# An attention and gated-convolution kernel: q and k of the first batch element in six tensors, the first w_in tile in one piece

## The chip, the cores and the metric

One core of a Trainium2 chip runs the program. The metric is the device time of one execution in microseconds (us), the median over runs; a profiled execution gives the trace. The engines are TensorE (PE), VectorE (DVE), ScalarE (ACT), GpSimd (POOL) and SyncE (SP), which here only issues DMAs.

## The reference

Block-causal attention (blocks of 64) over 8 batch elements, 8 heads, 576 positions and head size 64, and behind it a feed-forward layer with a gate from a convolution of three taps over positions:

```python
scores = scale * q @ k.T;  mask by blocks of 64;  attn = softmax(scores)
x = (attn @ v), heads side by side                      # 8 x 576 x 512
h = np.maximum(x @ w_in, 0.0)                           # 512 -> 1024
conv_out[s] = sum over j of conv_w[j] * h[s + j - 1]    # zero outside 0..575
gate = 1.0 / (1.0 + np.exp(-conv_out))
return (h * gate @ w_out).astype(np.float32)            # 1024 -> 512
```

q, k, v are float32. w_in, conv_w and w_out are float64: the kernel reads them as pairs of 32-bit words and puts float32 values together on the chip ("decode").

## The kernel before, in words

**Precision.** Most products run on pairs of a high part (type fp32r) and a low remainder: weights stand as wih and wil (w_in) and woh and wol (w_out). Heads are handled in pairs, four pairs per batch element.

**The decode of a weight tile** (function `split`, which calls `decode`). w_in has eight tiles of 128 columns, 512 KB each as 64-bit words. A tile is loaded (L1142), then: absolute value (ACT, L1013), clamp (L1019, POOL, for tile 0 DVE), a shift (DVE, L1024), the sign put in (DVE, L1036), a mask (DVE, L1040), then the high part (ACT, L1082) and a first low part (DVE, L1047). PE forms minus the high part and plus that low part in a bank (L1098, L1101), and DVE adds the value (L1104), which gives wil. Staging buffers gh and gl hold two tiles each. Before the change tile 0 is the one that is cut in two halves (`SHARE = {0: 2}`), so that each step of it runs twice on half the width; tile 1 comes first.

**The first batch element** is done in two visits per pair: "A" for its first 256 positions, for all four pairs, then "B" for the rest. The later elements are one visit per pair, 28 in all. For the A visits `load_first` fetches 256 positions of q and k of all pairs in twelve DMAs (L952): for q and for k a group for pair 0, one for pair 1 and one for pairs 2 and 3, each in two loads of 128 positions. The two loads of k for pair 0 go by ACT's queue, the rest by SP's. They all land in one tensor, seen under two types (`qkf`, `qkr`):

```python
qkt = [nc.alloc_sbuf_tensor_at(f"qk{x}", [P, 2, 2, H, D], d, offset=at0).ap() for x, d in (("f", F32), ("r", F32R))]
```

`first_t` then transposes a pair's q or k on PE (two matmuls, L1326) and ACT copies the result out (L840). Scores follow (L1578, with the mask L1582), row maxima (DVE, L1596), exponentials (ACT, L1604), sums and reciprocals (DVE, L1610, L1614), scaling (POOL, L1619), transposes of the probabilities (PE, L1665) and the product with v.

The feed-forward products are L1867 (w_in) and L1933 (w_out); they fill PE wherever attention leaves room.

**The order** is not written by hand. Every operation has a due time in a table of numbers (TARGETS), and `Plan.order` simulates the five engines with fixed costs per operation: on each engine the ready operation with the lowest due time goes next. Where the planner sees PE without work it puts in filler matmuls (L2085) whose result is not used. The planner knows for a transpose only the loads of its own group (`deps=lds[p]`). The semaphore waits are set by the framework from the tensors that an instruction reads and writes. DMA completions go round eight semaphores, so a DMA also waits until the one eight places before it has landed.

Of the kernel before, what the change touches and what calls it, by code (L numbers as in the profile page):

```python
# [11 lines left out]
F32 = mybir.dt.float32  # L12
F32R = mybir.dt.float32r
# [568 lines left out]
def kernel(  # L582
# [10 lines left out]
    nc = tc.nc  # L593
# [3 lines left out]
    P = 128  # L597
# [59 lines left out]
    VAT = (0, 1, None, 0)  # L657
    SRAW, PRA, PRB = True, True, (0, 1)
    FHP = ()
    ZDMA, APM, SHARE = True, True, {0: 2}  # L660
    LQ, LQS, LV, LVS = -60.0, 8.22, -56.75, 13.33
    WL0, WLS = -49.08, 2.41
    NEAR, FAR, BIAS = 0.0, 1.0, 0.0
# [277 lines left out]
    def load_first():  # L941
# [25 lines left out]
        for z in range(2):  # L967
            res.append((lambda z=z: qkt[1][:, z], bufs, lds[z]))
# [1153 lines left out]
```

## Time and profile before

| | us |
|---|---|
| median of 3 runs | 766.57 (766.47 to 767.78) |
| profiled execution | 767.02 |
| its span | 765.2 |
| PE busy | 748.2 (98% of the span) |
| DVE busy | 628.4 (82%) |
| ACT busy | 605.2 (79%) |
| POOL busy | 426.7 (56%) |

The span runs from the first to the last instruction. Matmuls overlap in the pipeline and the ends are modelled, so a busy PE is not a PE at its peak; fillers count as busy. A row of a stage gives each engine's busy time in that stretch, with the number of its instructions. The chain of waits is followed back from the last instruction and is shown in order of time: start, length, and what ran or landed. A row "A <- B: total, times, longest" is a wait of A for B. A row of a group gives the count, the busy time, the mean of one in ns and the idle time ahead.

### The profile page before, as it was taken

How to read it: one execution, taken by the hardware profiler on the slowest of the kernel's cores; microseconds unless marked ns; L12 is line 12 of the kernel's file. 1: busy time of each engine (PE TensorE's matmuls, PEld its weight loads, DVE VectorE, ACT ScalarE, POOL GpSimd, SP SyncE). 2: the span in 40 equal slices, each digit the busy share in tenths (PEclk: the TensorE clock that was granted, in tenths of full speed). 3: DMA queues.
4: the chain of work that ended last, by engine and by line, in shares of the span. 5: the costliest groups of instructions: out<-in, count | busy, mean ns of one | idle time of the engine just before them, and what ended most of it. 6: DMA issues, size and time to landing. Idle time of an engine off the chain costs nothing.

```text
span 765.2 us, 16814 instructions
## 1 busy us (share of the span) xinstructions
PE 748.2 (98%) x5175; PEld 672.3 (88%) x5175; DVE 628.4 (82%) x1840; ACT 605.2 (79%) x1754; POOL 426.7 (56%) x642
## 2 busy tenths in 40 slices
PE   6999999999999999999999999999999999999998
PEld 4666789989989899999989899898989899898997
DVE  3899999989978789898979789798888879786541
ACT  2888989978978679797978689798888768786652
POOL 1444765766755547576566547546566655564421
PEclk9999999999999999999999999999999999999999
DMA  7575574667544565645354663555456454440001
GB/s 198 149 181 149 126 167 116 152 163 167 127 104 113 126 144 120 142 113 136 94 135 113 142 151 93 136 124 130 103 117 156 106 147 102 95 102 15 14 29 42
DMA packets 165629, 92.64 MB, mean 121 GB/s; under 512 B 134924, under 2 KB 142116, under 8 KB 165540
## 3 DMA queue, kind: packets, MB, share of 16 engines
q1 hardware_dynamic: 164996, 91.43, 49.3%
q8 instruction: 42, 0.69, 0.4%
q14 instruction: 47, 0.39, 0.2%
q10 hardware_dynamic: 544, 0.13, 0.1%
HBM read 38.30 MB, written 9.44 MB: 62 GB/s over the span
## 4 chain that ended last, share of the span: by engine, by line
PE 77%; ACT 11%; DVE 5%; DMA 3%; issue 2%; POOL 1%; SPq 0%; ACTq 0%; DVEq 0%; POOLq 0%
PE bank L1933 25%; PE bank L1867 21%; PE bank L1785 10%; PE bank L1665 6%; PE bank L1470 4%; PE bank L1472 4%; PE bank L1423 3%; PE bank L1216 2%; DMA qkf<-in_k_dram 2%; DMA x<-in_moe_w_out_dram 2%; ACT ptbh L1676 1%; DVE st L1480 1%; ACT p4f L1439 1%; DVE t L1888 1%; ACT t L1884 1%
## 5 line engine op out<-in xcount | busy, mean ns | idle before, releaser
L1867 PE MATMUL bank<-x,wih 128*128 128x290 f32 (+3 forms) x1024 | 199.3, 299 | 0.0
L1907 POOL TENSOR_TENSOR gl<-t,gh 128x289 fp32r<-128x289 f32 (+3 forms) x128 | 104.1, 819 | 102.8 <-ACT gh L1904 97.4
L1867 PEld LDWEIGHTS bank<-x,wih 128*128 128x128 f32 x1024 | 157.6, 188 | 3.5 <-issue 0.4
L1933 PE MATMUL bank<-woh,gh 128*128 128x512 f32 (+1 forms) x296 | 118.2, 399 | 0.0
L1933 PE MATMUL bank<-wol,gh 128*128 128x512 f32 (+1 forms) x296 | 115.0, 389 | 0.0
L1933 PE MATMUL bank<-woh,gl 128*128 128x512 f32 (+1 forms) x296 | 114.9, 388 | 0.0
L1867 PE MATMUL bank<-x,wil 128*128 128x290 f32 (+3 forms) x512 | 110.7, 298 | 0.0
L1480 DVE TENSOR_REDUCE st<-bank 128x1 f32<-128x128 f32 (+3 forms) x224 | 106.5, 481 | 2.8
L1676 ACT ACTIVATE ptbh<-bank 128x384 fp32r<-128x384 f32 (+2 forms) x180 | 87.1, 503 | 11.6 <-PE bank L1665 10.7
L1679 DVE TENSOR_TENSOR ptbl<-bank,ptbh 128x512 fp32r<-128x512 f32 (+1 forms) x142 | 88.7, 632 | 8.0 <-ACT ptbh L1676 5.7
L1888 DVE SCALAR_TENSOR_TENSOR t<-bank,cw,t 128x289 f32<-128x289 f32 (+3 forms) x128 | 65.0, 509 | 25.6 <-ACT t L1884 25.1
L1867 PEld LDWEIGHTS bank<-x,wil 128*128 128x128 f32 x512 | 82.5, 188 | 1.0
L835 POOL TENSOR_SCALAR vv<-vn 128x320 fp32r<-128x320 f32 (+2 forms) x62 | 28.5, 461 | 82.1 <-DMA vn<-in_v_dram 29.3
L1472 PE MATMUL bank<-kl,qz 128*128 128x128 f32 (+2 forms) x224 | 71.7, 322 | 0.0
L1884 ACT ACTIVATE t<-bank,cw 128x289 f32<-128x289 f32 (+3 forms) x128 | 63.9, 500 | 5.0 <-POOL gl L1907 2.7
L1933 PEld LDWEIGHTS bank<-woh,gl 128*128 128x128 f32 x296 | 55.5, 188 | 12.5
L1892 DVE SCALAR_TENSOR_TENSOR t<-bank,cw,t 128x288 f32<-128x288 f32 (+3 forms) x128 | 64.5, 506 | 1.3
L1785 PE MATMUL bank<-ptbl,vv 128*64 128x192 f32 x240 | 64.5, 314 | 0.0
L1904 ACT ACTIVATE gh<-t 128x289 fp32r<-128x289 f32 (+3 forms) x128 | 56.7, 445 | 9.8 <-DVE t L1900 8.8
L1897 ACT ACTIVATE t<-t 128x289 f32<-128x289 f32 (+3 forms) x128 | 56.8, 444 | 8.9 <-DVE t L1892 8.2
L1881 ACT ACTIVATE bank<-bank 128x290 f32<-128x290 f32 (+3 forms) x128 | 51.6, 403 | 14.5 <-PE bank L1867 12.7
L1900 DVE SCALAR_TENSOR_TENSOR t<-t,bank 128x289 f32<-128x289 f32 (+3 forms) x128 | 57.0, 446 | 6.0 <-ACT t L1897 4.9
(183 smaller groups left out, 2013.4 us busy)
## 6 DMA issues: line engine op xcount, KB each, us to landing
out_dram<-stage SPq DMA_DIRECT2D x35, 256.0 KB, 2.3
ka<-kh SPq DMA_DIRECT2D x56, 144.0 KB, 2.6
kb<-kh SPq DMA_DIRECT2D x56, 144.0 KB, 2.6
vn<-in_v_dram SPq DMA_DIRECT2D x60, 128.0 KB, 2.7
qnf<-in_q_dram SPq DMA_DIRECT2D x56, 128.0 KB, 2.4
knf<-in_k_dram SPq DMA_DIRECT2D x56, 128.0 KB, 2.7
x<-in_moe_w_out_dram SPq DMA_DIRECT2D x8, 512.0 KB, 4.0
qz<-qh SPq DMA_DIRECT2D x28, 144.0 KB, 2.5
```

Source lines behind the costliest of these rows:

```text
L1472: nc.tensor.matmul(sb.ap[:, 0:nk], qz.ap[:, z:z + 128], kl.ap[:, 0:nk], start=False, stop=True)
L1480: nc.vector.tensor_reduce(out=st.ap[:, i:i + 1], in_=sb.ap[:, 0:nk], op=ALU.max, axis=AX.X, negate=True)
L1676: nc.scalar.activation(out=hi(), in_=src(), func=AF.Copy)
L1679: nc.vector.tensor_tensor(out=lo(), in0=src(), in1=hi(), op=ALU.subtract)
L1785: nc.tensor.matmul(tb.ap[0:m, q0 - qa:qb - qa], vv.ap[:, chunk(c), w[ps_]], pm.ap[:, 128 * c + q0:128 * c + qb] if qa == 0 else pm.ap[:, c ...
L1867: nc.tensor.matmul(fb.ap[:, 0:n2], wt[:, c, fs], xs[c][xi].ap[:, x0:x0 + n2], start=(n + c - c0 == 0), stop=(n + c - c0 == 3 * NCC - 1))
L1884: nc.scalar.activation(out=t.ap[:, 0:no], in_=fb.ap[:, own:own + no], func=AF.Copy, scale=cw[:, NFC + f:NFC + f + 1])
L1888: nc.vector.scalar_tensor_tensor(out=t.ap[:, i0:no], in0=fb.ap[:, own + i0 - 1:own + no - 1], scalar=cw[:, f:f + 1], in1=t.ap[:, i0:no], o ...
L1892: nc.vector.scalar_tensor_tensor(out=t.ap[:, 0:i1], in0=fb.ap[:, own + 1:own + 1 + i1], scalar=cw[:, 2 * NFC + f:2 * NFC + f + 1], in1=t.a ...
L1900: nc.vector.scalar_tensor_tensor(out=t.ap[:, 0:no], in0=t.ap[:, 0:no], scalar=1.0, in1=fb.ap[:, own:own + no], op0=ALU.add, op1=ALU.mult)
L1907: nc.gpsimd.tensor_tensor(out=gbuf[1].ap[:, f, carry:carry + no], in0=t.ap[:, 0:no], in1=gbuf[0].ap[:, f, carry:carry + no], op=ALU.subtract)
L1933: nc.tensor.matmul(fb.ap[:, 0:cut], gbuf[a].ap[:, f, cs], w[:, f, ds], start=(f == 0 and n == 0), stop=(f == NFC - 1 and n == 2))
```

## The change: six tensors, one piece, and another table of due times

The one tensor of q and k becomes six, each under two types: for q and for k one for pair 0, one for pair 1 and one for pairs 2 and 3. Loads and transposes address their own. They lie at the same place in memory, one behind the other. Tile 0 of w_in is no longer cut. TARGETS is another table of 6,414 numbers in place of 6,425, since the uncut tile has fewer operations. Below line 734 line numbers rise by five (L1326 becomes L1331).

```diff
-219 209 325 302 354 325 246 281 286 295 371 375 506 444 710 738 354 406 519 734 553 576 526 591 650 559 328 325 411 393 578 563 408 432 411 482 459 473 436
...
-    ZDMA, APM, SHARE = True, True, {0: 2}
+    ZDMA, APM, SHARE = True, True, {}
...
-    qkt = [nc.alloc_sbuf_tensor_at(f"qk{x}", [P, 2, 2, H, D], d, offset=at0).ap() for x, d in (("f", F32), ("r", F32R))]
+    qkt = [[[], []], [[], []]]
+    for z in range(2):
+        for p0, p1 in ((0, 1), (1, 2), (2, 4)):
+            for y, (x, d) in enumerate((("f", F32), ("r", F32R))):
+                qkt[y][z].append(nc.alloc_sbuf_tensor_at(f"qk{x}{z}{p0}", [P, 2, 2 * (p1 - p0), D], d, offset=at0).ap())
+            at0 += 4 * 4 * (p1 - p0) * D
...
-                        eng.dma_start(out=qkt[0][:, z, c, 2 * p0:2 * p1, :],
+                        eng.dma_start(out=qkt[0][z][g][:, c],
...
-            res.append((lambda z=z: qkt[1][:, z], bufs, lds[z]))
+            res.append((lambda z=z: qkt[1][z], bufs, lds[z]))
...
-                                     x()[:, c, 2 * p:2 * p + 2, :].rearrange("p j d -> p (j d)"), rident, start=(c == 0), stop=True,
+                                     x()[min(p, 2)][:, c, 2 * (p == 3):2 * (p == 3) + 2, :].rearrange("p j d -> p (j d)"), rident, start=(c == 0), stop=True,
```

**PE at the start.** Here is the start of PE's queue before, with the semaphores on which each instruction waits; DMAHW0 to DMAHW7 are the eight of the DMAs.

```order
L2085 MATMUL bank<-blank 128x512 x13
L1326 MATMUL bank<-rident,qkr 128x128 [waits DMAHW2_49,DMAHW3_49,DMAHW1_49,DMAHW4_49,DMAHW0_49,DMAHW7_49,DVE_49,PE_49]
L1326 MATMUL bank<-rident,qkr 128x128
L2085 MATMUL bank<-rident 128x512 x7
L1098 MATMUL bank<-wih,nident 128x512 [waits PE_49,Activation_49]
L1101 MATMUL bank<-wil,rident 128x512 [waits DVE_49]
L2085 MATMUL bank<-rident 128x512 [waits PE_49]
L2085 MATMUL bank<-rident 128x512 x2
L1098 MATMUL bank<-wih,nident 128x256 [waits PE_49,Activation_49]
L1326 MATMUL bank<-rident,qkr 128x128 [waits DMAHW3_49,DMAHW4_49,DMAHW2_49,DMAHW6_49,DMAHW0_49,DVE_49]
L1326 MATMUL bank<-rident,qkr 128x128 x3
L1578 MATMUL bank<-kh,qa 128x128 [waits Activation_49]
```

And now (qkr10 is k of pair 0, qkr00 q of pair 0, qkr01 q of pair 1):

```order
L2090 MATMUL bank_165<-blank_141 128x512 x17
L1103 MATMUL bank_208<-wih_136,nident_132 128x512 [waits PE_49,Activation_49]
L1331 MATMUL bank_211<-rident_130,qkr10_120 128x128 [waits DMAHW2_49,DMAHW0_49,DVE_49]
L1331 MATMUL bank_211<-rident_130,qkr10_120 128x128
L1106 MATMUL bank_208<-wil_137,rident_130 128x512 [waits DVE_49]
L2090 MATMUL bank_220<-rident_130 128x512 x5
L1103 MATMUL bank_233<-wih_136,nident_132 128x512 [waits DVE_49,Activation_49]
L1331 MATMUL bank_236<-rident_130,qkr00_114 128x128 [waits DMAHW6_49,DMAHW4_49,PE_49]
L1331 MATMUL bank_236<-rident_130,qkr00_114 128x128
L1106 MATMUL bank_233<-wil_137,rident_130 128x512 [waits DVE_49]
L1331 MATMUL bank_245<-rident_130,qkr01_116 128x128 [waits DMAHW7_49,DMAHW0_49,PE_49]
```

A transpose waits for two DMA semaphores instead of five or six, the fillers at the front are 18 instead of 14 (one more row of one stands ahead of each), and the transposes of q stand behind products of two w_in tiles. In all there are 34 fillers instead of 36.

**SP at the start.** SP's queue before, and behind it the queue now:

```order
L952 DMA qkf<-in_k_dram 128x2x64
L952 DMA qkf<-in_k_dram 128x2x64 [waits DMAHW0_49]
L952 DMA qkf<-in_q_dram 128x2x64 [waits DMAHW1_49]
L952 DMA qkf<-in_q_dram 128x2x64 [waits DMAHW2_49,PE_49]
L952 DMA qkf<-in_q_dram 128x4x64 [waits DMAHW3_49]
L952 DMA qkf<-in_q_dram 128x4x64 [waits DMAHW4_49]
L1184 DMA t<-in_moe_conv_w_dram 24x256 [waits DMAHW5_49]
```

```order
L1147 DMA gh<-in_moe_w_in_dram 128x4x256 x2
L957 DMA qkf_113<-in_q_dram 128x2x64
L1147 DMA gl<-in_moe_w_in_dram 128x4x256
L957 DMA qkf_113<-in_q_dram 128x2x64
L957 DMA qkf_115<-in_q_dram 128x2x64
L957 DMA qkf_115<-in_q_dram 128x2x64 [waits DMAHW0_49]
L1189 DMA t<-in_moe_conv_w_dram 24x256 [waits DMAHW1_49]
L957 DMA qkf_121<-in_k_dram 128x2x64 [waits DMAHW2_49]
L957 DMA qkf_121<-in_k_dram 128x2x64 [waits DMAHW3_49]
L957 DMA qkf_117<-in_q_dram 128x4x64 [waits DMAHW4_49]
```

The wait for PE at the fourth row of before is gone; the loads of q for pair 0 stand behind two and three whole w_in tiles (before, behind one; half a tile and another whole one followed). Further on, tile 7 of w_in waits in this queue for DVE, and the next loads of q and k for the B visits stand behind it.

**DVE at the start.** DVE's queue now, from the first w_in tile on:

```order
L1029 TENSOR_SCALAR gh<-gh 128x512
L1041 SCALAR_TENSOR_TENSOR gh<-gh 128x512
L1045 TENSOR_SCALAR gh<-gh 128x512
L1024 TENSOR_SCALAR gh<-gh 128x512
L1052 SCALAR_TENSOR_TENSOR wil<-gh 128x4x128
L1029 TENSOR_SCALAR gh<-gh 128x512
L1041 SCALAR_TENSOR_TENSOR gh<-gh 128x512
L1109 TENSOR_TENSOR wil<-bank,gh 128x4x128
L1045 TENSOR_SCALAR gh<-gh 128x512
L1052 SCALAR_TENSOR_TENSOR wil<-gh 128x4x128
L1109 TENSOR_TENSOR wil<-bank,gh 128x4x128
L1029 TENSOR_SCALAR gl<-gl 128x512
```

The steps of the first two tiles are woven together and both stand ahead of the third (gl); before, the second set was half of tile 0, its last step stood behind the first two maxima of pair 0, and tile 0's other half followed behind tile 3.

More of the change, by code (lines that the diff above doesn't have):

```diff
@@ L949, in load_first, with go @@
                 for c in range(2):
-                    def go(src=src, z=z, c=c, p0=p0, p1=p1):
+                    def go(src=src, z=z, c=c, p0=p0, p1=p1, g=g):
                         eng = nc.scalar if src is k and p0 == 0 else nc.sync
-                        eng.dma_start(out=qkt[0][:, z, c, 2 * p0:2 * p1, :],
+                        eng.dma_start(out=qkt[0][z][g][:, c],
                                       in_=src[0, 2 * p0:2 * p1, 128 * c:128 * c + 128, :].rearrange("h p d -> p h d"))
@@ L1326, in tr @@
                     nc.tensor.matmul(tb.ap[:, c * P:(c + 1) * P].bitcast(F32R),
-                                     x()[:, c, 2 * p:2 * p + 2, :].rearrange("p j d -> p (j d)"), rident, start=(c == 0), stop=True,
+                                     x()[min(p, 2)][:, c, 2 * (p == 3):2 * (p == 3) + 2, :].rearrange("p j d -> p (j d)"), rident, start=(c == 0), stop=True,
                                      is_transpose=True, skip_group_check=True)
```

435 rows, old and new, of the table TARGETS are left out of this document.

## The prediction

> **What bounds the kernel now.** I read the page's sums first, then the stages, then the chain of waits at the start.
>
> ```profile
> span 765.2 us, 16814 instructions
> PE 748.2 (98%) x5175; PEld 672.3 (88%) x5175; DVE 628.4 (82%) x1840; ACT 605.2 (79%) x1754; POOL 426.7 (56%) x642
> 0.00:20.00 20.00, 12.45 (x46) 9.12 (x47) 6.36 (x22) 5.70 (x12) 2.20 (x8) 0.90 0.72 200
> 20.00:45.00 25.00, 23.34 (x142) 15.30 (x142) 22.82 (x68) 22.50 (x74) 10.63 (x23) 0.95 0.65 174
> 45.00:60.00 15.00, 14.84 (x91) 10.36 (x91) 14.21 (x35) 12.96 (x38) 6.68 (x9) 1.00 0.66 167
> 60.00:100.00 40.00, 38.53 (x255) 29.38 (x254) 36.50 (x94) 35.73 (x102) 24.45 (x36) 1.00 0.54 135
> 100.00:700.00 600.00, 596.81 (x4269) 551.95 (x4268) 523.97 (x1573) 497.05 (x1456) 365.09 (x547) 1.00 0.52 124
> 0.00:20.00 20.00, 9.56 (x24) 6.81 (x24) 0.90 0.72 200
> 20.00:45.00 25.00, 5.27 (x12) 2.66 (x12) 0.95 0.65 174
> ```
>
> The first two lines are the page's; then stages with, after the length, the busy time of PE, PEld, DVE, ACT and POOL, the granted clock, the DMA share and GB/s; the last two count the filler matmuls (L2085) alone. From 100 to 700 us PE is busy 596.81 of 600, so the end is PE's work plus whatever PE loses before. It loses nearly all at the start: in 0 to 100 us it idles 100 - 89.16 = 10.84 us (the four stages sum to 89.16) and runs 9.56 + 5.27 = 14.83 us of fillers, 25.7 us together. In the first 20 us DVE works 6.36 and ACT 5.70 us; from 20 to 45 us DVE works 22.82 and ACT 22.50 of 25. So the start is slow because something late keeps DVE and ACT from their backlog. The chain says what:
>
> ```profile
> 0.73 3.78 DMA qkf<-in_k_dram
> 4.53 4.39 DMA qkf<-in_k_dram
> 9.42 0.48 PE bank L1326 x2
> 9.91 0.37 SPq L952
> ...
> 12.92 4.71 DMA qkf<-in_k_dram
> 17.72 0.36 PE bank L1326 x2
> PE bank L1326 <- DMA qkf<-in_k_dram: 6.0, 2, 3.3
> SPq L952 <- PE bank L1326: 4.4, 1, 4.4
> ```
>
> Columns: start, length; in the two wait rows the total, the times, the longest. The first transposes (L1326, pair 0's q) run at 9.42, just behind a load of k for pair 1 that lands at 4.53 + 4.39 = 8.92, though their own q stands second in SP's queue. SP's next q load waits for these transposes (4.4 us), so everything behind it in SP's queue leaves from 9.91 on. The second transposes wait for the last of all twelve loads, 12.92 + 4.71 = 17.63. Both rows fit one cause: q and k are one tensor, so a reader waits for every load issued to it, and a load waits for every reader.
>
> **The change part by part.** *Six tensors.* Each transpose now waits for its own two loads, and no q or k load waits for PE. PE's 6.0 us and SP's 4.4 us go. What is late next are loads, or the weight decode that PE's queue has ahead of the transposes. These rows price it:
>
> ```profile
> 2.00:4.00 2.00, 2.00 (x6) 1.54 (x5) 0.00 (x0) 1.10 (x1) 0.00 (x0) 1.00 0.91 277
> 4.00:6.00 2.00, 2.00 (x6) 1.53 (x6) 0.00 (x0) 1.02 (x3) 0.35 (x1) 1.00 1.06 251
> 6.00:8.00 2.00, 0.65 (x3) 0.19 (x1) 1.54 (x3) 0.00 (x0) 0.26 (x1) 1.00 1.03 316
> 1.05 5.60 PE L2085 MATMUL bank<-blank 128*128 128x512 f32 x14 [1.05 <-DVE blank L829]
> 6.76 0.69 DVE L1036 SCALAR_TENSOR_TENSOR gh<-gh 128x512 int32<-128x512 int32 x1
> 7.55 0.43 DVE L1040 TENSOR_SCALAR gh<-gh 128x512 int32<-128x512 int32 x1
> 10.53 0.62 ACT L1082 ACTIVATE wih<-gh 128x512 fp32r<-128x512 f32 x1
> 10.87 0.69 DVE L1047 SCALAR_TENSOR_TENSOR wil<-gh 128x512 fp32r<-128x512 uint32 x1
> 13.29 0.69 DVE L1104 TENSOR_TENSOR wil<-bank,gh 128x512 fp32r<-128x512 f32 x1 [1.07 <-PE bank L1101]
> 18.54 0.49 PE L1578 MATMUL bank<-kh,qa 64*128 64x128 f32 x4 [0.31 <-ACT kh L840]
> 24.19 1.13 DVE L1596 TENSOR_REDUCE st<-bank 128x1 f32<-128x128 f32 x4
> 24.28 0.38 POOL L1619 TENSOR_SCALAR p0f<-p0f,st 128x128 f32<-128x128 f32 x1 [11.58 <-DVE t L1040]
> 24.63 0.48 POOL L1619 TENSOR_SCALAR p1f<-p1f,st 128x256 f32<-128x256 f32 x1
> 24.95 0.25 PE L1665 MATMUL bank<-rident,p0r 128*128 128x128 f32 x1 [0.15 <-ACT qa L840]
> 27.52 0.57 ACT p1f L1604 x2
> 28.16 0.35 ACT p0f L1604 x2
> ```
>
> Loads: the first three rows move 554 + 502 + 632 KB by 8 us. Ahead of pair 0's second q load now stand k (128 KB), three whole w_in tiles (1,536) and half of q (64), so with its own 64 it is done after 1,792 KB, about 8.5 us; pair 1's q at 9.0 and k at 9.7, pair 2's q at about 11. The second tile is there after 1,152 KB, at 6.5.
>
> PE's queue: 18 fillers now stand first; at 5.60/14 = 0.40 each they end near 8.3. Then two decodes are woven in. DVE has the first tile's steps at the times shown until 7.98; then come, by the shown lengths, the second tile's clamp (0.43) to 8.4, the first's low part (0.69) to 9.1, and the second's steps (0.43, 0.69) to 10.2, its high part on ACT (0.62) to 10.9, DVE's remainder of the first (0.69) to 10.9, then 0.43 and 0.69 for the second's low part to 12.05. PE's second low product follows, pair 1's q, and pair 0's scores at about 12.9: **5.6 us before 18.54**. DVE then has the second remainder, two steps of the third tile and a small one (0.69 + 0.43 + 0.20 + 0.69, the 0.20 estimated from the steps above at their smaller size) to 14.6, four maxima (1.13) to 15.7; ACT's four exponentials end near 17.3, at 0.57 or 0.35 each (the last two rows, pieces of the chain, are two such passes); sums and reciprocals (0.3) and POOL's two scalings (0.38 + 0.48) give the transposes of pair 0's probabilities at 18.5: **6.4 us before 24.95**. I carry 6.4, since behind it ACT and DVE are full.
>
> *One piece for the tile.* Half-tile rows against whole-tile rows (count, busy, mean ns):
>
> ```profile
> L1036 DVE SCALAR_TENSOR_TENSOR gh<-gh 128x256 int32<-128x256 int32 x2 | 0.8, 422 | 0.0
> L1104 DVE TENSOR_TENSOR wil<-bank,gh 128x256 fp32r<-128x256 f32 x2 | 0.8, 418 | 0.4 <-PE bank L1101 0.4
> L1024 DVE TENSOR_SCALAR gh<-gh 128x256 int32<-128x256 int32 x2 | 0.6, 286 | 0.0
> L1024 DVE TENSOR_SCALAR gh<-gh 128x512 int32<-128x512 int32 x3 | 1.3, 420 | 4.7 <-POOL gh L1019 4.7
> ```
>
> Three of the six DVE steps cost 0.42 a half, three 0.29: 2 x (3 x 0.42 + 3 x 0.29) = 4.26; whole, 3 x 0.69 + 3 x 0.42 = 3.33. DVE saves 0.9, of which up to 0.9 and at least nothing reaches the end; I take 0.4, since DVE and ACT share the bound from 20 to 45 us. PE's columns stay the same. One DMA falls away on SP, which then has slack: 0, at most its 0.5 us of issue if SP were late.
>
> *The searched order.* It moves instructions on every engine to the end, not at the start alone. Between 100 and 700 us PE idles 3.2 us; removing it all is the best there, 8.8 us more (the slower rival, below) the worst; I take 0.4 given back, near the present idle, since the same rules of planning made both orders. Sum: 6.4 + 0.4 - 0.4 = 6.4. Cross-check by PE's account: 8.3 to the end of the front, 16 later fillers (22 before, so 9.2 us by 14.83 - 5.60) at 0.42 = 6.7, other idle as before (10.84 - 6.0 - 1.05 = 3.8), 18.8 against 25.7: 6.9.
>
> The profiled execution took 767.02 with its span of 765.2; 767.0 - 6.4 = 760.6. It stands 0.45 over the median 766.57, so the forecast is **760.2**.
>
> [...] The loads of the first 60 us are 200 x 20 + 174 x 25 + 167 x 15 = 10.9 MB; with 6.4 us less they need 203 GB/s instead of 181. The row of 6 to 8 us has 316, so I leave the sum as it is. [...]
>
> **The rivals.** *Given back* (0.22): the lead is real at 18 us, but something eats 1 to 5 us of it before PE is full: the loads, or SP's in-order queue, in which w_in tile 7 waits for DVE with the next q and k behind it. For it: DVE's 22.82 of 25, so that any late load stalls a full engine. Against it:
>
> ```profile
> SPq L859 <- PE bank L1216: 7.4, 2, 6.9
> ```
>
> SP stood still for 6.9 us in that stage now, and no PE wait of more than 1 us answers to it. Gain 3: 763.6 by the median. *More* (0.07): the whole 0.9 of the decode counts, and the new order also takes out half of the 3.2 us of later idle: gain 6.4 + 0.9 + 1.6, 757.7. *Slower* (0.08): the new order leaves bubbles in the steady stage. Its price is in one row:
>
> ```profile
> PE bank L1216 <- ACT p4f L1439: 1.1, 1, 1.1
> ```
>
> That is one missed hand-over in the 28 visits of whole head pairs. If ACT's last softmax block comes that late in 8 or more pairs besides, 8 x 1.1 = 8.8 beats 6.4: 769.0. Against it: PE idles 0.5% there now, with the same planner's rules. *The wait stays* (0.03): if the six tensors, which share memory with later buffers, were still held as one, PE would keep 6.0 and time stays within 0.2%, 766.6.
>
> **How the numbers follow.** The forecast, gain 5.5 to 7.5, has 0.60 (759.1 to 761.1 by the median). A measurement can tell about 0.2%, 1.5 us. Faster: 0.60 + 0.22 + 0.07 = 0.89, less 0.01 for a lead wholly given back: 0.88; same 0.03 + 0.01 = 0.04; slower 0.08. The range 757.2 to 764.8 holds the forecast, most of "given back" and most of "more", and leaves out slower and no change.
>
> **What would show it.** Right: no wait of L1331 (L1326 now) on k loads beyond 1 us; no SP wait on PE before 12 us; pair 0's scores near 12.9 and probability transposes near 18.5; DVE over 10 us busy in the first 20; 6 to 7 us less PE idle plus fillers before 100 us; the later stages as before. Wrong: transposes still at 17 us; or scores early and PE idle returning between 20 and 60 us; or more than 5 us idle from 100 to 700 us.

## The result and the profile after

The changed kernel takes **754.82 us** (median of 3 runs, 754.38 to 755.61) against 766.57 before, a ratio of 0.9835 with a 95% interval of 0.9805 to 0.9865. That is 11.75 us faster. The forecast was 760.2 us with a range of 757.2 to 764.8: the direction and the place were right, the gain was nearly twice the 6.4 us that the sum gave, and the time lies 2.4 us below the range. The profiled execution took 754.82 us with a span of 753.0.

The page's sums of the kernel after:

```profile
span 753.0 us, 16770 instructions
PE 744.2 (99%) x5171; PEld 667.7 (89%) x5171; DVE 627.2 (83%) x1834; ACT 603.4 (80%) x1752; POOL 427.9 (57%) x642
```

Its stages (length, then the busy time and count of PE, PEld, DVE, ACT and POOL, the granted clock, the DMA share and GB/s):

```profile
0.00:20.00 20.00, 16.75 (x89) 11.90 (x90) 12.87 (x41) 11.66 (x33) 4.78 (x14) 1.00 0.92 244
20.00:45.00 25.00, 23.88 (x147) 15.43 (x146) 23.80 (x63) 24.52 (x76) 15.78 (x23) 1.00 0.59 161
45.00:60.00 15.00, 14.64 (x90) 10.00 (x89) 13.79 (x35) 11.73 (x32) 5.74 (x8) 1.00 0.72 194
60.00:100.00 40.00, 39.85 (x265) 31.67 (x265) 37.73 (x97) 36.13 (x102) 23.11 (x34) 1.00 0.55 141
100.00:700.00 600.00, 599.07 (x4281) 553.31 (x4280) 517.54 (x1557) 491.60 (x1442) 364.06 (x546) 1.00 0.52 123
```

The same for the fillers alone (now L2090; the columns of DVE, ACT and POOL fall away):

```profile
0.00:20.00 20.00, 8.86 (x26) 6.31 (x26) 1.00 0.92 244
20.00:45.00 25.00, 2.88 (x8) 1.27 (x8) 1.00 0.59 161
```

Three things are to be seen. DVE works 12.87 us in the first 20 instead of 6.36, so its backlog starts early. PE idles 0.93 us from 100 to 700 us instead of 3.19. And the granted clock is 1.00 in both first stages, where it was 0.90 and 0.95; the sum of the prediction had no term for that.

PE's account closes on the span. PE's idle time and fillers before 100 us fall from 25.67 to 16.62 us: idle 3.25 + 1.12 + 0.36 + 0.15 = 4.88 (20 - 16.75 and so on), fillers 8.86 + 2.88 = 11.74. That is 9.05 us less. From 100 to 700 us there are 2.26 us less idle. PE's other work, busy time less fillers, falls from 748.2 - 14.83 = 733.4 to 744.2 - 11.74 = 732.5 us, 0.9 less. The tail behind 700 us is the same, 3.0 us idle in both. The sum is 12.2, the difference of the spans (765.2 - 753.0).

The timeline of PE and DVE at the start (start, length, engine, line, operation, tiles; x is the count, so that a row's length is that of the group):

```profile
1.05 6.44 PE L2090 MATMUL bank<-blank 128*128 128x512 f32 x18 [1.05 <-DVE blank L834]
8.72 0.29 PE L1331 MATMUL bank<-rident,qkr 128*128 128x128 f32 x2
9.27 1.32 PE L2090 MATMUL bank<-rident 128*128 128x512 f32 x5
11.01 0.29 PE L1331 MATMUL bank<-rident,qkr 128*128 128x128 f32 x2
12.22 0.49 PE L1583 MATMUL bank<-kh,qa 64*128 64x128 f32 x4
13.88 1.13 DVE L1601 TENSOR_REDUCE st<-bank 128x1 f32<-128x256 f32 x4
17.46 0.25 PE L1670 MATMUL bank<-rident,p0r 128*128 128x128 f32 x1
```

Pair 0's scores stand at 12.22 (18.54 before, forecast 12.9), its probability transposes at 17.46 (24.95 before, forecast 18.5). The front's fillers end at 7.49 (forecast 8.3).

The waits of the kernel after (total, times, longest): the two longest of PE in the first 100 us, PE's only two from 100 us on, and the longest of SP's queue in the first 60 us:

```profile
PE bank L2090 <- DVE blank L834: 1.1, 1, 1.1
PE bank L1103 <- ACT wih L1087: 0.9, 1, 0.9
PE bank L1475 <- ACT p3f L1488: 0.4, 1, 0.4
PE bank L1670 <- DVE bank L1482: 0.2, 1, 0.2
SPq L1378 <- ACT kh L845: 2.6, 1, 2.6
```

No wait of L1331 for a load is among PE's, and none of SP's load issues waits for the transposes.

### The profile page after: what moved, and what is told of

Same layout as the page of the kernel before. It is cut to its first block, busy times and chain, and to the rows that moved or that the text cites. A ratio compares the mean times of both kernels' runs of the same rounds, so it can differ in the third digit from the quotient of the medians.

```text
span 753.0 us, 16770 instructions
## 1 busy us (share of the span) xinstructions
PE 744.2 (99%) x5171; PEld 667.7 (89%) x5171; DVE 627.2 (83%) x1834; ACT 603.4 (80%) x1752; POOL 427.9 (57%) x642
## 4 chain that ended last, share of the span: by engine, by line
PE 85%; ACT 4%; DVE 4%; DMA 3%; SPq 2%; issue 1%; POOL 0%; POOLq 0%; ACTq 0%; DVEq 0%
PE bank L1938 26%; PE bank L1872 25%; PE bank L1790 11%; PE bank L1670 7%; PE bank L1477 4%; PE bank L1475 4%; PE bank L1428 3%; PE bank L1221 2%; DMA gh<-in_moe_w_in_dram 2%; SPq L1282 1%; PE bank L1766 1%; DMA vn<-in_v_dram 1%; DVE st L1538 1%; ACT ptbh L845 1%; DMA gl<-in_moe_w_in_dram 0%
## 5 line engine op out<-in xcount | busy, mean ns | idle before, releaser
L1485 DVE TENSOR_REDUCE st<-bank 128x1 f32<-128x128 f32 (+1 forms) x224 | 105.9, 480 | 2.9
L1477 PE MATMUL bank<-kl,qz 128*128 128x128 f32 (+1 forms) x224 | 71.6, 322 | 0.0
L1813 DVE TENSOR_TENSOR xt<-bank,xt 64x256 f32<-64x256 f32 (+1 forms) x112 | 51.6, 460 | 14.6 <-ACT xt L1810 11.4
```

The costliest lines, as they stand in the source:

```text
L1477: nc.tensor.matmul(sb.ap[:, 0:nk], qz.ap[:, z:z + 128], kl.ap[:, 0:nk], start=False, stop=True)
L1485: nc.vector.tensor_reduce(out=st.ap[:, i:i + 1], in_=sb.ap[:, 0:nk], op=ALU.max, axis=AX.X, negate=True)
```

## The experiments

All times are medians of up to 12 runs, all ratios are against runs of the kernel before on the same chip, with 95% intervals. The kernel before had medians of 766.78, 765.63, 768.15 and 766.87 us in the four comparisons, so ratios are compared rather than microseconds.

**The change again.** It was timed once more beside the experiments, with no edit.

> The changed kernel once more, for a tighter interval beside the others: 754 to 756. Every theory expects the same.

754.36 us (754.27 to 754.78), ratio 0.9849 [0.9835, 0.9863]. The gain is 1.5 to 1.65%. The front of its profile differs from the first one's:

```profile
1.05 6.90 PE L2090 MATMUL bank<-blank 128*128 128x512 f32 x18 [1.05 <-DVE blank L834]
8.85 0.28 PE L1331 MATMUL bank<-rident,qkr 128*128 128x128 f32 x2
```

The same 18 fillers take 6.90 us instead of 6.44 and end at 7.96 instead of 7.49, yet the first transposes stand only 0.13 us later and pair 0's probability transposes 0.09 (17.55). PE's idle time and fillers before 100 us are 4.15 + 12.19 = 16.34 us here, beside 16.62.

**Six tensors alone.** The old table, tile 0 in halves.

```diff
-    ZDMA, APM, SHARE = True, True, {}
+    ZDMA, APM, SHARE = True, True, {0: 2}
...
-TARGETS = (the change's table)
+TARGETS = (the table before)
```

(as an edit of the changed kernel, which makes the kernel before with the code of the split)

> Before with the six tensors alone: its own table of due times and the tile in two halves stay. Theory A (the one tensor's waits are the cause): PE's 6.0 us wait of L1326 on k loads and SP's 4.4 us wait on PE vanish, the time falls by 5 to 7 us, to 760 to 762. Rival B (the new table of due times makes the gain, whatever the tensors): no more than 1.5 us, 765 or more. If A alone were everything, 755.

757.31 us (756.66 to 761.18), ratio 0.9887 [0.9869, 0.9905]. The split alone brings 1.1%, 8.7 us of 766.6: most of the gain, and more than the 5 to 7 us expected. Both waits are gone from its profile (which is of the longest of its five runs, 761.18): the first transposes stand at 5.95 us, and pair 0's probability transposes at 16.72, 8.2 us earlier than before.

**One tensor with the rest of the change.** The new table and the whole tile, q and k in one tensor.

```diff
-    qkt = [[[], []], [[], []]]
-    for z in range(2):
-        for p0, p1 in ((0, 1), (1, 2), (2, 4)):
-            for y, (x, d) in enumerate((("f", F32), ("r", F32R))):
-                qkt[y][z].append(nc.alloc_sbuf_tensor_at(f"qk{x}{z}{p0}", [P, 2, 2 * (p1 - p0), D], d, offset=at0).ap())
-            at0 += 4 * 4 * (p1 - p0) * D
+    qkt = [nc.alloc_sbuf_tensor_at(f"qk{x}", [P, 2, 2, H, D], d, offset=at0).ap() for x, d in (("f", F32), ("r", F32R))]
...
```

(the loads and the transposes are addressed as before)

> The change without the six tensors: q and k in one tensor again, with the new table and the whole tile. Theory A: the transposes wait again for all loads issued to the tensor before them, and one SP load waits for PE; PE loses 4 us or more at the start, time 759 to 766. Rival B: 755 to 757, as the new order alone gives the gain.

763.52 us (761.95 to 768.45), ratio 0.9965 [0.9947, 0.9982]. Its waits of PE in the first 60 us:

```profile
PE bank L1326 <- DMA qkf<-in_k_dram: 3.9, 1, 3.9
PE bank L1326 <- DMA qkf<-in_q_dram: 1.8, 1, 1.8
```

Its stages from 10 to 30 us:

```profile
10.00:20.00 10.00, 5.33 (x22) 3.94 (x24) 2.86 (x8) 2.44 (x6) 0.97 (x1) 0.56 0.79 208
20.00:30.00 10.00, 9.63 (x48) 6.73 (x47) 6.93 (x22) 5.56 (x21) 2.63 (x6) 0.50 0.77 232
```

The wait for foreign loads is back, 5.7 us in two pieces, and from 10 to 30 us the granted clock is about half. The profiled execution took 767.52 us, though, and its clock is not that of most runs: four of the twelve took 767.0 to 768.5 us with a mean granted clock of 0.982 to 0.984, eight took 762.0 to 764.0 us with 0.991 to 0.993. Without the split the table and the tile are worth 0.35%, 2.7 us (0.5% by those eight runs); with it (0.9887 to 0.9835 or 0.9849) 0.38 to 0.52%, 2.9 to 4.0 us. The two bundles add up almost without remainder.

**Which tensor boundary does it.** The kernel before with three tensors, q and k of a group together, and with two, all of q and all of k; old table and halves in both. The first edit:

```diff
-    qkt = [nc.alloc_sbuf_tensor_at(f"qk{x}", [P, 2, 2, H, D], d, offset=at0).ap() for x, d in (("f", F32), ("r", F32R))]
+    qkt = [[[], []], [[], []]]
+    for p0, p1 in ((0, 1), (1, 2), (2, 4)):
+        for y, (x, d) in enumerate((("f", F32), ("r", F32R))):
+            pair = nc.alloc_sbuf_tensor_at(f"qk{x}{p0}", [P, 2, 2, 2 * (p1 - p0), D], d, offset=at0).ap()
+            for z in range(2):
+                qkt[y][z].append(pair[:, z])
+        at0 += 8 * 4 * (p1 - p0) * D
...
```

(loads and transposes address their own, as in the change)

> The kernel before with three tensors instead of one: the loads of q and of k that belong to one pair of heads share a tensor; the old order, tile 0 in two pieces. The first transposes then wait for pair 0's loads alone, and no load waits for PE. Theory W (what the split into six gains is that the first transposes no longer wait for other pairs' loads, and that the loads behind no longer wait for PE): nearly all of the six tensors' gain, 757 to 759 us, the first transpose at 6 to 7.5 us and pair 0's probability transposes at 16.5 to 18. Rival N (the gain needs q and k apart, so that PE can begin on k while q is under way): half of it, 761 to 763 us.

759.36 us (758.57 to 761.47), ratio 0.9896 [0.9877, 0.9914], where six tensors had 0.9887. The second edit:

```diff
+    for z in range(2):
+        for y, (x, d) in enumerate((("f", F32), ("r", F32R))):
+            whole = nc.alloc_sbuf_tensor_at(f"qk{x}{z}", [P, 2, H, D], d, offset=at0).ap()
+            for p0, p1 in ((0, 1), (1, 2), (2, 4)):
+                qkt[y][z].append(whole[:, :, 2 * p0:2 * p1])
+        at0 += 4 * 2 * H * D
...
```

> The kernel before with two tensors, all of q in one and all of k in the other; the old order, tile 0 in two pieces. Here the waits stay: the first transposes wait for all pairs' loads of q or of k issued before them, and a later load still waits for PE. Theory W: close to the kernel before, 763 to 767 us, the first transpose at 8.5 us or later. Rival M (more tensors help by themselves, whichever wait they leave, e.g. through fewer semaphores on the way): 759 to 762 us.

768.14 us (766.47 to 769.42), ratio 1.0002 [0.9989, 1.0014]: nothing. Its waits of PE and of SP's queue (L1332 are the transposes, L958 the loads):

```profile
PE bank L1332 <- DMA qkf<-in_k_dram: 2.8, 1, 2.8
PE bank L1332 <- issue: 2.5, 1, 2.5
SPq L958 <- PE bank L1332: 4.4, 1, 4.4
```

SP's 4.4 us are those of the kernel before, to the digit. The first transposes come at 9.54 us (before, 9.42); for the 2.5 us ahead of them the profile names no releaser. With three tensors none of these rows is there, the first transposes stand at 6.16 and pair 0's probability transposes at 16.76, as the first theory had it, and two rows of the stages stand nearly as in the kernel with six (17.63 and 23.50 us of PE):

```profile
0.00:20.00 20.00, 17.77 (x97) 12.46 (x97) 13.45 (x45) 12.14 (x36) 5.47 (x15) 1.00 0.85 222
20.00:45.00 25.00, 23.52 (x151) 16.09 (x151) 23.34 (x64) 23.93 (x74) 12.66 (x22) 1.00 0.70 184
```

So a second tensor does nothing by itself; a boundary between the pairs does nearly all, since it is the other pairs' loads that are late. That q and k are apart adds nothing that can be told with the old table. The same edit in the changed kernel, with its own table and the whole tile:

> The change with three tensors instead of six: q and k of one group share one, all else as in the change. Theory W: the first transposes, of pair 0's k, wait for pair 0's q too, and both are there before PE has ended the first product of w_in (q landed at 8.80 us in the change, the transposes of k ran at 8.72), so the time is the change's, 754 to 756 us. Rival N (q and k have to be apart): 757 us or more.

756.45 us (754.63 to 759.72), ratio 0.9861 [0.9841, 0.9882]. It lies between the two expectations, and its interval takes in the change's 0.9849. Its transposes of pair 0's k stand at 9.06 us (8.72 in the change), but in this profile the clock of 10 to 20 us is 0.83, as it isn't in the change's. Two of the five runs have a mean granted clock of 1.000 and took 754.63 and 755.35 us, the change's time; the other three, at 0.998, 0.997 and 0.993, took 756.45, 757.15 and 759.72. All seven runs of the change are at 0.999 or 1.000. So where the clock holds, q and k apart seem worth nothing here too; whether they help to hold it five runs can't tell.

**The clock alone.** What the kernel of this case loses in its waits besides the waits themselves is seen in its own profile: the stages from 10 to 30 us of the kernel before, in the columns of the stages above.

```profile
10.00:20.00 10.00, 6.26 (x30) 4.41 (x30) 4.28 (x11) 3.32 (x8) 0.88 (x1) 0.84 0.81 222
20.00:30.00 10.00, 9.50 (x56) 6.45 (x56) 8.75 (x29) 7.80 (x28) 3.89 (x8) 0.87 0.78 228
```

Its timeline behind the first wait (start, length, engine, line, operation, tiles, count, and in brackets the idle time ahead):

```profile
9.42 0.47 PE L1326 MATMUL bank<-rident,qkr 128*128 128x128 f32 x2 [2.77 <-DMA qkf<-in_k_dram]
9.68 3.12 PE L2085 MATMUL bank<-rident 128*128 128x512 f32 x7
```

Seven fillers behind the 2.77 us of idle time take 3.12 us, 0.45 each; in the changed kernel five of the same shape take 1.32, 0.26 each. The experiment keeps every wait and every load and fills the two waits with 11 and 14 more fillers:

```diff
+        k += {0: 11, 2: 14}.get(len(fills), 0)
         fills.append(k)
```

> The kernel before with 25 more empty matmuls, all in PE's two waits for loads of q and k: 11 behind the 14 at the front, 14 behind the three ahead of tile 0's half. The waits themselves stay as they are. Theory C (a part of what the split of the tensor gains is TensorE's clock, which the two waits lose): with PE kept busy, later fillers of the start stand 0.23 us apart instead of 0.43, the granted clock from 10 to 30 us is 1.00 instead of 0.84 and 0.87, and the time falls by 1 to 2.5 us, ratio 0.997 to 0.9985. Rival N (the clock costs nothing here, since PE waits at the start anyway): within 0.1% of the kernel before, or slower where a filler holds up work.

765.27 us (762.9 to 767.78) against 766.87, ratio 0.9973 [0.996, 0.9987]. 25 additional instructions that compute nothing make the kernel 0.27% faster, 2.1 us with an interval of 1.0 to 3.1. Its eleven runs have a mean granted clock of 0.997 to 1.000, the sixteen of the kernel before beside them 0.993 to 0.996. Its timeline at the same place:

```profile
9.60 0.34 PE L1326 MATMUL bank<-rident,qkr 128*128 128x128 f32 x2 [1.14 <-DMA qkf<-in_k_dram]
9.78 1.83 PE L2086 MATMUL bank<-rident 128*128 128x512 f32 x7
```

Its stages from 10 to 30 us:

```profile
10.00:20.00 10.00, 8.51 (x47) 6.42 (x47) 4.54 (x12) 3.55 (x9) 0.89 (x1) 1.00 0.86 227
20.00:30.00 10.00, 9.15 (x62) 6.03 (x62) 9.42 (x31) 8.60 (x31) 5.03 (x10) 1.00 0.76 224
```

The wait of SP's queue for the transposes:

```profile
SPq L952 <- PE bank L1326: 4.5, 1, 4.5
```

The same seven fillers take 1.83 us instead of 3.12, the clock is 1.00 throughout, and SP's wait of 4.5 us is still there. So about 2 of the split's 8.7 us are the clock, an estimate that takes it to be worth as much beside the earlier loads; the rest, by difference, is what the earlier loads bring.

**The later fillers left out.** The changed kernel with the 18 fillers at the front alone; the other 16 aren't issued.

```diff
-        def go():
+        def go(first=len(fills) == 1):
+            if not first:
+                return
```

> The change with the 18 fillers of the front and without the 16 later ones, all other instructions in the same order. PE spends 11.74 us on fillers in the first 45 us, some 5.3 of it on the later ones. If they only fill time in which PE would wait (theory): 754 to 756. If they stand ahead of useful work that is ready: 751 to 753. If they keep the clock up and it falls without them: 757 or more.

757.37 us (756.33 to 758.93), ratio 0.989 [0.9874, 0.9907], against 0.9849: about 3 us slower for less work. Its stages from 10 to 30 us:

```profile
10.00:20.00 10.00, 7.33 (x53) 5.26 (x53) 8.69 (x26) 7.28 (x23) 3.46 (x7) 0.87 1.04 258
20.00:30.00 10.00, 8.90 (x47) 5.46 (x43) 7.82 (x20) 8.51 (x29) 3.14 (x6) 0.78 0.75 245
```

PE idles 2.67 and 1.10 us there instead of 1.31 and 0.32, and the clock falls to 0.87 and 0.78; over a whole run it is 0.989 to 0.995 in all five. The later fillers, 5.3 us of PE's time, hold the clock and cost less than they save.

**A longer front.** The changed kernel with 36 fillers ahead of the first transposes instead of 18.

```diff
-            for _ in range(k):
+            for _ in range(k + 18 * (x is blank)):
```

> The change with 36 instead of 18 empty matmuls ahead of the first transposes, some 6 us more of them, of which about 1.2 us fall into PE's present wait for the first load; the start is then 4 to 5 us later and all else is as in the change. Theory P (PE is the bound all along, so a start that is later by some time ends later by as much): 758 to 760 us, with PE's idle time after 45 us within 1 us of the change's. Rival S (the stages behind have slack, which takes up a good part of a late start): 754.5 to 756.5 us.

758.36 us (758.13 to 758.61), ratio 0.9874 [0.9858, 0.9891]. In its profile the first transposes stand at 12.59 us, 3.87 later than in the change, and the span is 756.7, 3.7 longer. Its stage from 100 to 700 us:

```profile
100.00:700.00 600.00, 599.25 (x4280) 553.05 (x4279) 520.83 (x1564) 492.55 (x1447) 361.45 (x544) 1.00 0.52 123
```

PE idles 0.75 us there (0.93 in the change), and 1.81 us in all behind 45 us (1.44). In these two traces nothing behind takes the delay up: what is lost at the start is lost at the end. The ratios say it less firmly. This kernel ran on another chip than the change, beside runs of the kernel before of 768.15 us; against 0.9849 or 0.9835 its 0.9874 is 0.25 to 0.39%, 1.9 to 3.0 us, of the 3.87, and either difference is uncertain by 2 us or so. On the scale of 766.57 it would be 756.9 us, between the two expectations. What speaks for P is the trace.

The same profile has the fillers alone in stretches of 2 us (busy time and count of PE and PEld, clock, DMA share, GB/s):

```profile
1.00:3.00 2.00, 1.95 (x5) 1.58 (x6) 1.00 0.40 116
7.00:9.00 2.00, 2.00 (x10) 1.63 (x9) 1.00 1.14 264
```

In 2 us stand first 5 and then 10 fillers of one shape, at a granted clock that reads 1.00 both times. The pace changes at 6.7 us; this trace has no record of the clock before 6.62 us, and the row counts what has no record as 1.00.

**The whole tile in the old table.** The kernel before with the tile whole and its table without the eleven numbers of the second half; and the same with six tensors.

```diff
-    ZDMA, APM, SHARE = True, True, {0: 2}
+    ZDMA, APM, SHARE = True, True, {}
...
-TARGETS = (the table before, 6,425 numbers)
+TARGETS = (the table before without its numbers 59 to 69)
```

> The kernel before with one edit of the change: w_in tile 0 is loaded and decoded in one piece; one tensor for q and k and the old order (without the eleven numbers of the second piece). By the fourth run, in which the whole tile in the old order gained nothing behind six tensors, 765 to 768 us, no change that can be told. By the rival, that fewer VectorE instructions in the start count by themselves (0.9 us in the profile of before, 3.6 us in the comparison of the change with the half tiles in the new order), 762 to 765 us.

770.59 us (768.06 to 775.01), ratio 1.0035 [1.0018, 1.0051]: slower by 2.7 us, which neither expectation had.

> Six tensors and the whole tile with the old table (the eleven numbers of the second half dropped). Theory A with the tile at 0.4 to 0.9 us: 759 to 761. Rival C (the tile matters more, by taking half a decode out of the full stage from 20 to 45 us): 757 or less. Rival B: 764 or more. What it leaves against the change's 754.8 is the table's share.

760.59 us (759.34 to 761.98), ratio 0.9918 [0.9906, 0.993]; the six tensors in the old table with halves had 0.9887. The fillers alone of the kernel with one tensor and the whole tile:

```profile
0.00:20.00 20.00, 11.35 (x29) 8.07 (x29) 0.91 0.69 190
20.00:45.00 25.00, 5.97 (x19) 3.33 (x19) 0.93 0.60 168
```

The two stages hold 48 fillers instead of 36 and 17.32 us of them instead of 14.83, and the probability transposes come at 28.91 us instead of 24.95 (with six tensors at 18.69 instead of 16.72). So the start gets longer, and the decode that the one piece saves on DVE is not what counts there.

**Half tiles in the new table.** Six tensors; the eleven numbers of the second half put into the change's table.

```diff
-    ZDMA, APM, SHARE = True, True, {}
+    ZDMA, APM, SHARE = True, True, {0: 2}
...
-TARGETS = (the change's table, 6,414 numbers)
+TARGETS = (the change's table, and in it, behind number 58, the eleven of the table before)
```

> Six tensors with the new table, but tile 0 in two halves; the second half gets the eleven numbers that it had before. Theory: the whole tile saves DVE 0.9 us, of which 0.4 to 0.9 count: 755.3 to 756. Rival (the whole tile is what lets the start keep ACT and DVE full): 757 or more. Rival (the halves bring the first data earlier and are no worse): 754.8 or less.

757.97 us (757.63 to 758.08), ratio 0.9895 [0.988, 0.9909]. With these the ratios make a table:

| | old table | new table |
|---|---|---|
| one tensor, halves | 1 | not run |
| one tensor, whole tile | 1.0035 | 0.9965 |
| six tensors, halves | 0.9887 | 0.9895 |
| six tensors, whole tile | 0.9918 | 0.9835, 0.9849 |

The split is worth 1.13%, 1.17% and 1.16 to 1.30% (1.0 to 1.1 by the eight runs named above) in the three places where it can be read: within the intervals it doesn't depend on the rest. The tile costs 0.31 to 0.35% in the old table and is worth 0.46 to 0.60% in the new one; the new table is worth nothing with halves (0.08% slower) and 0.69 to 0.83% with the whole tile. Neither has a price of its own. A caution on this: the two mixed kernels run a table that was not made for their number of operations, so the 0.3% that they lose may be the misfit rather than the tile.

**The new table by halves of the program.** Six tensors, the whole tile. The numbers of the two tables under 2000 are due times in the first 100 us (20 to the microsecond). One kernel takes these from the change and all later ones from the table before; the other the reverse.

```diff
-TARGETS = (the change's table)
+TARGETS = (n if n < 2000 else o, for each number n of the change's and o of the old table)
```

> The change with the old table's numbers for every operation that the new table puts at 100 us or later. By PE's account of the two traces 2.3 us of PE idle between 100 and 700 us went away, and 9.0 us of idle and fillers before 100. If that stage gain belongs to the later order: 757. If the start carries all and the later gaps were chance of how the start leaves the engines: 754 to 755.5.

758.0 us (757.71 to 758.46), ratio 0.9883 [0.9871, 0.9896]: 0.34 to 0.48% slower than the change, by a later order alone. Its profile's span is 756.2, 3.2 us longer than the change's. Of these only 1.0 is idle time from 100 to 700 us (1.95 against 0.93, row below); 2.3 is busy time: PE's work without fillers is 746.54 - 11.77 = 734.8 us here, 732.5 in the change, for the same matmuls in another order. Why they take longer in that order isn't shown.

```diff
-TARGETS = (the change's table)
+TARGETS = (o if n < 2000 else n)
```

> Six tensors and the whole tile, with the old numbers for operations that the new table puts before 100 us and the new numbers from there on; the counterpart of e5. e4 (all old) took 760.6, e5 (new start) 758.0, the change 754.8. If the later order is worth 3.2 us by itself, as e5 says: 757 to 758. If the later numbers only fit behind the new start: 760 or more.

759.89 us (758.78 to 762.0), ratio 0.9924 [0.9908, 0.994]: no better than the old table throughout (0.9918), against what the other half seemed to say. From 100 to 700 us, first the kernel with six tensors alone:

```profile
100.00:700.00 600.00, 595.50 (x4241) 549.95 (x4240) 518.16 (x1554) 490.50 (x1436) 360.08 (x540) 1.00 0.52 123
```

The new start with the old later order:

```profile
100.00:700.00 600.00, 598.05 (x4253) 551.34 (x4253) 517.51 (x1550) 489.55 (x1436) 359.50 (x539) 1.00 0.52 122
```

The old start with the new later order:

```profile
100.00:700.00 600.00, 599.15 (x4277) 552.45 (x4275) 523.65 (x1570) 495.00 (x1454) 364.33 (x549) 1.00 0.52 123
```

The idle time there goes with the later table: 0.93 us in the change, 0.85 with the new later order behind the old start, and 0.47 to 0.86 in the other kernels with the new one (change again, one tensor, three tensors, halves, front fillers, longer front); 1.95 to 4.50 in every kernel with the old one. So the new later order kept PE from idling in the last kernel too. In its profiled execution that gain was lost in the start, which has this stage:

```profile
20.00:30.00 10.00, 9.85 (x46) 6.54 (x46) 6.99 (x19) 7.41 (x24) 4.22 (x9) 0.58 0.82 253
```

PE is busy 9.85 of 10 us at a clock of 0.58. PE's work without fillers is 736.3 us in that execution against 734.0 in the kernel with the old table throughout, whose clock stays at 1.00. But the profiled execution (762.0) is this kernel's longest, and only it and one more of the six runs (761.3) have a mean granted clock below 1.000, 0.993 and 0.995. The four at 1.000 took 758.78 to 760.06 us, a median of 759.5, which is 0.992 of the kernel before beside them and still no better than the old table throughout. So the clock explains the two longest runs and not the median. Why it fell there, where PE idled 0.72 us from 20 to 45, and why the other four gain nothing by their ratio, is open.

## Why the prediction fell short, point by point

**What bounds the kernel: right.** PE's work sets the end and the start is what it loses. In the traces the longer front shows it (3.87 us later, 3.7 us longer; by the ratios 1.9 to 3.0), and the gain came from where it was looked for: 9.05 of 12.2 us of the span lie before 100 us.

**The cause of the waits: right.** In this kernel readers of one tensor wait for all its loads (6.0 us before), and loads for its readers (4.4 us). The two splits that differ in the boundary alone (0.9896 and 1.0002) show it.

**Six tensors: the mechanism right, the term of 6.4 mis-sized; it measured 8.7 alone** (0.9887). The 6.4 was the lead at pair 0's probability transposes, and in the trace of the change that lead is 7.5 (24.95 to 17.46). The failed step is the path to them: it was added up from rows laid end to end. In the trace DVE and ACT do it like this:

```profile
7.86 0.42 DVE L1024 TENSOR_SCALAR gh<-gh 128x512 f32<-128x512 f32 x1
8.20 0.69 DVE L1052 SCALAR_TENSOR_TENSOR wil<-gh 128x512 fp32r<-128x512 uint32 x1
8.80 0.42 DVE L1029 TENSOR_SCALAR gh<-gh 128x512 int32<-128x512 int32 x1
14.53 0.47 ACT L1609 ACTIVATE p1f<-bank,st 128x256 f32<-128x256 f32 x1
15.86 0.36 ACT L1609 ACTIVATE p0f<-bank,st 128x128 f32<-128x128 f32 x1
```

A step of DVE starts up to 0.09 us before the one ahead of it has ended (7.86 + 0.42 = 8.28, and the next starts at 8.20). So the second tile's low part ends at 11.61 (forecast 12.05), the scores stand at 12.22 (12.9), and ACT's exponentials, which begin at 14.53 beside DVE's maxima, end near 16.2 (17.3). That makes the lead 1.1 us larger than the sum's in the change's order; with the split alone, in the old order, the transposes stand at 16.72, a lead of 8.2.

The sum also had no term for TensorE's clock: the rows of 0.90 and 0.95 that it quoted went up to 1.00, and holding the clock alone was worth 2.1 us in the kernel before.

The cross-check priced 18 fillers at 5.60/14 = 0.40 us each and 16 later ones at 0.42. But of the fillers at the front the first eleven of the kernel before start mostly 0.43 us apart (up to 5.48 us) and the rest 0.23, so that a mean of the row is no price for one more: with the pace changing at nearly the same place (5.6 and 5.5 us), four more made the front 0.84 us longer (5.60 to 6.44), 0.21 each, and the 16 later ones take (8.86 + 2.88 - 6.44)/16 = 0.33. The account reads 7.5 to the front's end (8.3), 5.3 for the later fillers (6.7) and 3.8 of other idle time (4.88 less the 1.05 ahead of the front; 3.8 was the forecast), 16.6 in place of 18.8, so a gain before 100 us of 9.05 instead of 6.9. In this trace the difference is the price of fillers alone, but part of that is chance. In six traces with 18 fillers at the front they took 5.94 to 7.25 us, and the longest of these is the forecast's (8.3 less 1.05). In the second trace of the change the account is 8.0, 5.3 and 3.1, so that its difference is in part idle time. Nor did the front set the start: PE waits 0.9 us for ACT's wih behind it. (In the kernels with the split alone the gain before 100 us is 7.7 and 7.8 us.)

What sets TensorE's clock isn't shown. The fillers stand 0.43 us apart first and then 0.23, and the pace changed 2.9 to 6.2 us after the first filler in the sixteen traces, though all begin alike. In the kernel before, 2.77 us of idle time had seven fillers at 0.45 us each behind them, with a granted clock of 0.50 from 10 to 12 us; with the waits filled, 1.14 us of idle time at the same place had seven at 0.26 each behind them, at 1.00. How long a wait has to be for the clock to fall these runs don't tell.

**The sum stopped too early.** At pair 0's probability transposes the lead is 7.5 us, and at 100 us it is 9.05. The forecast stopped at the transposes, "since behind it ACT and DVE are full", and gave no credit for idle time later: from 45 to 100 us it fell from 1.63 to 0.51.

**One piece for the tile and the searched order: wrong as two terms, and the larger part of the miss.** The forecast had 0.4 gained and 0.4 given back. Together they measured 0.35 to 0.52%, 2.7 to 4.0 us, and neither has a price without the other. Of the change's profile, 2.26 us are idle time from 100 to 700 us, of the 3.19 that the forecast named as the most that was to be had there. The argument that "the same rules of planning made both orders" was the failed step here: the rules are the same, but each table of numbers brings its own idle time, 0.5 to 0.9 us for the one in seven kernels and 2.0 to 4.5 for the other. The bounds stood there, 3.2 better and 8.8 worse; the value between them had no row behind it.

**The rivals.** *Given back* didn't happen: the lead grew from 18 to 100 us. The loads do come faster, 244 GB/s in the first 20 us, and 244 x 20 + 161 x 25 + 194 x 15 = 11.8 MB in 60 us, 197 GB/s where the forecast asked for 203; SP's longest wait there is 2.6 us. A lead wholly given back, for which the chances have 0.01, no run shows: these loads came at 197 GB/s instead of the 181 of before. *More* was the right kind (the tile and half of the later idle time) and still too small, since it had 6.4 for the split. *Slower* fell: PE's waits behind 100 us are two of 0.4 and 0.2 us, 0.93 us of idle time in all. *The wait stays* fell with the first row.

**The signs.** All but two came: no wait of L1331 for loads, none of SP for the transposes, scores at 12.22, probability transposes at 17.46, DVE 12.87 us in the first 20. "6 to 7 us less PE idle plus fillers before 100 us" was exceeded (9.05), and "the later stages as before" was wrong in the kernel's favour.

## What to carry to other kernels

Where several loads fill one buffer that different steps read, cut it where the steps part, and not elsewhere: here a boundary between the pairs was worth 1.1% and one between q and k nothing. Steps of DVE that follow each other closely overlapped by up to 0.09 us here, so rows laid end to end made a path too long. Price one more instruction by the spacing at the place where it will stand, not by the mean of a group that spans two paces (here 0.43 and 0.23 us), and look at a wait of TensorE twice: for its length (2.77 us in the kernel before), and for slower matmuls behind it (there seven fillers at 0.45 us each instead of 0.26). A new order made by the same planner is not a term of zero: its idle time in the steady stage is to be bounded, and an edit that was planned together with its order is to be priced together with it.

## What the runs showed that was not expected

- Matmuls that compute nothing made a kernel faster: 25 of them in two waits gave 0.9973 [0.996, 0.9987], and 16 of them left out cost about 3 us (0.9849 to 0.989), with the clock from 10 to 30 us at 0.87 and 0.78.
- The first matmuls of the program ran at about half the later pace, 0.43 us apart instead of 0.23: eleven in the traces before and after, thirteen in the second trace of the change, seven to fifteen in all sixteen traces, though the program begins alike in each. The granted clock reads 1.00 there because the trace's first record of the clock comes with the change of pace (5.54 us in the change, 6.54 in its second trace, 3.99 to 7.24 in all). Before that the spacing of equal matmuls tells the pace, and the clock's column doesn't.
- A cut of one tile that was worth something in one order (0.46 to 0.60%) cost 0.31 to 0.35% in another (with a table that was not made for it), and the split of a tensor was worth much the same, 1.0 to 1.3%, in all of them.
